# The order of the first burst of each unit: one score product and one transposed score product change places

## The chip, the cores and the metric

One NeuronCore of a Trainium2 chip runs the whole program in one launch. The metric is the device time in microseconds (us) of that core; of several runs the median counts. A core has a matrix engine (TensorE: PE for its matmuls, PEld for its weight loads), a vector engine (VectorE, DVE), a scalar engine (ScalarE, ACT), GpSimd (POOL), and a queue of its own for DMA transfers (SyncE, SP). Each has its own list of instructions and waits for the others by semaphores.

## What is computed

A transformer layer with attention and MLP side by side on one normalised input, 2048 rows of 512 values, 32 heads of 16:

```python
def _A_ref(x, wqkv, wo):
    qkv = (x @ wqkv).reshape(B, S, 3, H, Dh).transpose(2, 0, 3, 1, 4)
    q, k, v = qkv[0], qkv[1], qkv[2]
    scores = jnp.einsum("bhqd,bhkd->bhqk", q, k) * (Dh ** -0.5)
    p = _softmax(scores, axis=-1)
    o = jnp.einsum("bhqk,bhkd->bhqd", p, v)
    return o.transpose(0, 2, 1, 3).reshape(B, S, D) @ wo

def _B_ref(x, w1, b1, w2, b2):
    h = _gelu(jnp.einsum("bsd,df->bsf", x, w1) + b1)
    return jnp.einsum("bsf,fd->bsd", h, w2) + b2

xn = _layernorm(x)
return x + _A_ref(xn, wqkv, wo) + _B_ref(xn, w1, b1, w2, b2)
```

## The kernel before

The attention is cut into 8 groups of 4 heads (`NG`), 4 blocks of 512 queries (`NQB`) and 16 steps of 128 keys, so there are `NU` = 512 units. `unit(gen)` (line 745) writes the instructions of one unit. It works on two units at once: on unit u it takes the row maxima of the scores (queries on the partitions), and on unit e = u - 19 (`LEAD`) it does the softmax proper with the scores transposed (keys on the partitions). The maxima of a whole block of queries have to be known before its exponentials.

Three kinds of attention product stand in a unit, each for four heads n = 0 to 3:

- `s_half(u, n)`, line 366: the score product of head n into a PSUM bank named pS, and behind it on VectorE the row maximum (`s_max`, line 363, `mt<-pS` in the profile). Below it is called s0, s1, s2 or s3.
- `e_half(e, n)`, line 399: the transposed score product into a bank named pT, and behind it on ScalarE the exponential (line 410, `pe<-pT`). Below: e0 to e3.
- `v_half(w, r)`, line 413: the product of the exponentials with the values, for all four heads, summed in one bank named pV over 16 units. Line 436 copies it out on ScalarE (`osb<-pV`).

All of them use half the rows of the matrix array. Heads 0 and 2 use the low half (rows 0 to 63), heads 1 and 3 the high half (rows 64 to 127). Line 169 issues every product as four matmuls of 32 columns each (`tiled`, line 195), so eight small matmuls can be under way at once, four on each half. `v_half` takes one half of the rows in each half of a unit, and `dense` takes the other half of the rows: it issues three or four products on that half (`pace`) for whatever else has to be multiplied, which is the projection of q, k, v, the two MLP products and the output projection. These are the pD rows of the profile; each product is again four matmuls of 32 columns.

So a unit has two halves, a = 0 and a = 1, and each is a burst of four score products, then the values, then the dense products:

| | burst, in the order of the program | then |
|---|---|---|
| a = 0 | s0 (low), e1 (high), s1 (high), e0 (low) | values on high, dense on low |
| a = 1 | s2 (low), e3 (high), s3 (high), e2 (low) | values on low, dense on high |

Three things set waits around a burst. The first is the banks (line 102): scores rotate over three banks and transposed scores over three, so a product waits until the maximum or the exponential that read its bank three products earlier has ended. When a dense group ends and a new one begins, `dbank` (line 513) takes one of the T banks for it, and the bank of the old group joins the T banks only when ScalarE has read it (for the first MLP product in line 1312, `hh<-pD`). Until then the transposed scores have two banks. The values do the same with an S bank every 16 units.

The second is the `turns` semaphore (lines 167 to 194): values and dense products add into the same bank from both row halves in turn, so the first of them in a burst waits until the last of them in the burst before has ended. A dense group that is over is left out of that count.

The third is that all matmuls of TensorE count up one semaphore, in the order of the program. VectorE's maximum of s0 and ScalarE's exponential of e1 both wait for that count to reach a number.

Of the kernel before, what the change touches and what calls it, by code (L numbers as in the profile page):

```python
# [54 lines left out]
def layer_kernel(ctx: ExitStack, tc: tile.TileContext, x, wqkv, wo, w1, b1, w2, b2, out):  # L55
# [51 lines left out]
    def banks(tag):  # L107
        k = free_banks[tag].pop(0)
        free_banks[tag].append(k)
        return bank_tile(k, tag)  # L110
# [48 lines left out]
    def given(engine, ns):  # L159
        backlog[engine] += ns  # L160
# [17 lines left out]
    def leave(user, goes_on):  # L178

        p = newest.pop(user, None)  # L180
        if p is not None and goes_on:
            p.then_inc(turns, 1)
            tc.no_tile_sem_insts.add(p.ins.name)
            counted[0] += 1
            left.append(p)

    def enter():

        if left:
            goal[0] = f"turn{counted[0]}"  # L190
            for p in left:
                tc.add_to_no_dep_group(goal[0], p.ins)
            left.clear()

    def tiled(user, dst, lhs, rhs, start, stop):

        for j in range(0, P, 32):
            product(user, dst[j:j + 32], lhs[:, j:j + 32], rhs, start=start, stop=stop)
# [11 lines left out]
    def fetch_scale(m):  # L210

        scale_of[m] = nc.scalar.alloc_register(f"sexp{m}")
        nc.scalar.reg_load(scale_of[m], sexp[0:1, m:m + 1].bitcast(I32))

    class Plan:
# [7 lines left out]
        def add(self, engine, ns, fn, after=(), take=(), free=(), size=0, tail=0, gap=0):  # L223
            t = dict(gap=gap, e=engine, ns=ns, fn=fn, after=[a for a in after if a], take=take, free=free, size=size, tail=tail,
                     end=None, n=len(self.todo))
            for key in free:
                self.users.setdefault(key, []).append(t)
            self.todo.append(t)
            return t
# [89 lines left out]
    def tick():  # L319
        held[0] = pos[0] < NU and pos[0] % 16 == 0  # L320
        run_due()
        run_steps()
        slot[0] += 1
# [42 lines left out]
    def s_half(u, n):  # L366

        s = banks("S")
        s_mm(u, n, s)
        s_max(u, n, s)  # L370

    def s_end(u):

        t, i = divmod(u, 16)
        if i < 15:
            return
        g, qb = divmod(t, NQB)
        mneg = mnegs[t % 2]
        nc.vector.tensor_reduce(mneg[:, :16], mt_of[t].rearrange("p h t k -> p (h t) k"), axis=AX.X, op=ALU.max, negate=True)
        given("dve", 220)  # L380

        def store():

            pt = banks("S")
            for a in range(2):
                nc.tensor.matmul(pt[32 * a:32 * a + 32, :64], mneg[64 * a:64 * a + 64, :],
                                 ident[64 * a:64 * a + 64, 64 * a:64 * a + 64], start=True, stop=True)
            mhl = work.tile([64, 2, 64], F16, name="mhl", bufs=2)
            nc.vector.tensor_scalar_mul(mhl[:, 0], pt[:64, :64], 1.0 / MROW)
            nc.vector.scalar_tensor_tensor(mhl[:, 1], pt[:64, :64], 1.0 / MROW, mhl[:, 0], op0=ALU.mult, op1=ALU.subtract)  # L390
            given("dve", 300)
            for a in range(2):
                nc.sync.dma_start(m_d[t, :, :, 64 * a:64 * a + 64], mhl[32 * a:32 * a + 16])
            for h in range(4):
                m_rows(t, h)

        stores[t] = store

    def e_half(u, n):

        p, a = divmod(n, 2)
        t, kt = divmod(u, 16)
        g, qb = divmod(t, NQB)
        st = banks("T")
        r = slice(64 * a, 64 * a + 64)
        k0 = (kt % 4) * P
        tiled(None, st, kst[g % 2][kt // 4][r, p, k0:k0 + P], qst[g % 2][qb][r, p, :], True, True)
        pe = work.tile([P, QB], F32, name="pe", bufs=12)
        ptiles[u, n] = pe
        nc.scalar.activation(pe, st, AF.Exp, scale=scale_of[g // 2])  # L410
        given("act", 520)

    def v_half(u, a):

        t, kt = divmod(u, 16)
        g, qb = divmod(t, NQB)
        if kt == 0 and a == 0:
            pv_of[t] = hold("V", "S")
        pv = pv_of[t][0]
        r = slice(64 * a, 64 * a + 64)  # L420
        for h in (2, 3, 0, 1):
            c = (4 * g + h) * VW
            product("V", pv[32 * h:32 * h + 32, :], vv[r, kt, c:c + 32], ptiles[u, h][r],
                    start=(kt == 0 and a == 0), stop=(kt == 15 and a == 1))
# [77 lines left out]
    NU = NG * NQB * 16  # L502
# [155 lines left out]
    def ended(at_once=True):  # L658

        if cur[0] is not None and cur[0].over():  # L660
            done, cur[0] = cur[0], None
            ends.append(done.end)
            if at_once:
                settle()
# [5 lines left out]
    def one_more():  # L670

        if ends:
            ends.pop(0)()
        elif extras:
            extras.pop(0)()
# [10 lines left out]
    def dense(gen, side):  # L686

        f = group(gen)
        for _ in range(0 if f is None else f.pace[pos[0] % 2]):
            if not f.usable(side):  # L690
                return
            f.product(side)
# [25 lines left out]
    def spare(gen, side):  # L718

        if extra[0] is None and not spent[0]:  # L720
            f = next(gen, 0)
            spent[0] = f == 0
            extra[0] = Halves(f) if f else None
        if extra[0] is not None:
            extra[0].product(side)
            if extra[0].at == extra[0].n:
                extra[0] = None
# [17 lines left out]
    def unit(gen):  # L745


        u = pos[0]
        e = u - LEAD
        if e > 0 and e % (2 * NQB * 16) == 0 and e < NU:  # L750
            fetch_scale(e // (2 * NQB * 16))
        pos[0] += 1
        for a in range(2):
            for b in range(2 * a, 2 * a + 2):
                if u < NU:
                    s_half(u, b)
                elif u > NU:
                    spare(gen, b % 2)
                if 0 <= e < NU:
                    e_half(e, b ^ 1)  # L760
            if e >= 0:
                one_more()
                enter()

                w, r = (e - 2, 1) if a == 0 else (e - 1, 0)
                live = 0 <= w < NU
                new = r == 0 and w % 16 == 0
                if live and not new:
                    v_half(w, r)
                dense(gen, 1 - r)  # L770
                if live and new:
                    v_half(w, r)

                for user, goes_on in (("V", live and not (r == 1 and w % 16 == 15)),
                                      ("D", cur[0] is not None and not cur[0].over())):
                    leave(user, goes_on)
                for k in backlog:
                    backlog[k] = max(0, backlog[k] - HALF)
                if live and r == 1:
                    v_end(w)  # L780
                ended(False)

            if a == 0 and u % 16 == 0 and u // 16 - 1 in stores:
                stores.pop(u // 16 - 1)()
        if u < NU:
            s_end(u)
        tick()
# [9 lines left out]
    with ExitStack() as st1:  # L797
# [252 lines left out]
        for w in (1, 0):  # L1050
# [5 lines left out]
            else:  # L1056
                a = add("POOL", 800, lambda wf=wf, i1=i1: nc.gpsimd.tensor_scalar(tl[wf], tl[wf], i1, 0.0, op0=ALU.mult, op1=ALU.add), [h])
                w_ready[w] = add("POOL", 1100, lambda wf=wf, hi=hi, lo=lo: nc.gpsimd.tensor_tensor(lo, tl[wf], hi, op=ALU.subtract), [a], free=[wf])
        a = add("DVE", 90, lambda: nc.vector.tensor_tensor(sexp[:, 0:1], fac0[:, 0:1], fac0[:, 1:2], op=ALU.mult), [chain])
        a = add("DVE", 90, lambda: nc.vector.tensor_scalar_mul(sexp[:, 0:1], sexp[:, 0:1], DH ** -0.5), [a])  # L1060
# [5 lines left out]
        a = add("DVE", 90, lambda: nc.vector.tensor_tensor(amv[:, 2:3], amv[:, 0:1], amv[:, 1:2], op=ALU.max), v_sum)  # L1066
# [3 lines left out]
        for i in range(2):  # L1070
# [6 lines left out]
            else:  # L1077
                b = add("POOL", 1240, lambda key=key: nc.gpsimd.tensor_scalar(
                    tl[key], tl[key], inv_v[:, 0:1], 0.0, op0=ALU.mult, op1=ALU.add), [h])
# [30 lines left out]
        a = add("DVE", 220, maxima, m_last)  # L1110
# [3 lines left out]
        def turn_m():  # L1114
            tl[mkey] = sb_tile(mkey)
            for k in range(2):
# [3 lines left out]
        a = add("PE", 300, turn_m, [a], take=[mkey])  # L1120
        a = add("DVE", 160, lambda: nc.vector.tensor_scalar_mul(mhl[:, 0], tl[mkey][:64, :64], 1.0 / MROW), [a])
        a = add("DVE", 160, lambda: nc.vector.scalar_tensor_tensor(mhl[:, 1], tl[mkey][:64, :64], 1.0 / MROW, mhl[:, 0],
                                                                   op0=ALU.mult, op1=ALU.subtract), [a], free=[mkey])
# [371 lines left out]
```

## Time and profile before

| | |
|---|---|
| median of 3 runs | 1487.3 us (1486.66 to 1488.96) |
| the profiled execution, by its own time | 1485.57 us |
| its span, from the first to the last instruction | 1483.8 us |
| granted TensorE clock, mean | 0.997 |
| VectorE busy | 1374.5 us (93%), 2029 row maxima in it |
| ScalarE busy | 1259.2 us (85%), 2048 exponentials in it |
| GpSimd busy | 662.2 us (45%) |

Busy shares are unions over time of the instructions of an engine. For PE the ends of matmuls are modelled by the profiler, and a busy PE says nothing on its two row halves, of which one can stand still. A timeline row merges instructions of one kind that follow each other: start, length from the first start to the last end, engine, source line, the tiles, and xN for their number; in brackets stands idle time of the engine ahead of it and what ended it. Of the 2048 row maxima 2029 read a bank named pS; the other 19, of the prologue, read one named pV.

### The profile page before, as it was taken

To read this page: it belongs to the slowest core of one execution; us is meant where nothing else is said; L and a number is where in the kernel's file an instruction comes from. 1 tells how busy PE (TensorE), PEld (TensorE's weight loads), DVE (VectorE), ACT (ScalarE), POOL (GpSimd) and SP (SyncE) were. 2 spreads that over 40 slices of the span, in tenths; PEclk is the share of its full clock that TensorE was granted. 3 is DMA by queue.
4 is the path that set the end of the run, shared out by engine and by line. 5 is a ranking of instruction groups with operands and counts; after the bars stand their busy time and mean duration, and the time that the engine had idled before them with its cause. 6 is when DMAs were issued, how large, how long until landed. Compare 5 with 4: busy or idle time off the path is not lost.

```text
span 1483.8 us, 88118 instructions
## 1 busy us (share of the span) xinstructions
PE 1467.1 (99%) x40158; PEld 811.5 (55%) x40158; DVE 1374.5 (93%) x2305; ACT 1259.2 (85%) x2366; POOL 662.2 (45%) x672
## 2 busy tenths in 40 slices
PE   8999999999999999999999999999999999999998
PEld 4445555555555555555555555555555555555554
DVE  7889999999999999999999999999999999999923
ACT  5868888888999888899988889998888998888884
POOL 3202857563787301377831037782115777121100
PEclk9999999999999999999999999999999999999999
DMA  6732556554224210221112111121112110111432
GB/s 213 226 113 70 163 171 195 160 157 144 76 72 114 65 37 23 68 62 41 44 43 87 30 36 44 53 73 44 43 38 80 50 37 21 56 55 31 141 93 95
DMA packets 112623, 124.83 MB, mean 84 GB/s; under 512 B 22908, under 2 KB 84220, under 8 KB 112248
## 3 DMA queue, kind: packets, MB, share of 16 engines
q1 hardware_dynamic: 112248, 119.18, 26.6%
q8 instruction: 314, 5.14, 1.5%
q14 instruction: 61, 0.50, 0.1%
HBM read 81.66 MB, written 37.34 MB: 80 GB/s over the span
## 4 chain that ended last, share of the span: by engine, by line
PE 89%; DVE 8%; ACT 1%; DMA 1%; issue 0%; SPq 0%; DVEq 0%; ACTq 0%
PE pV L169 26%; PE pD L169 25%; PE pS L169 18%; PE pT L169 18%; DVE mt L363 7%; PE pT L992 2%; DMA wq<-in_A_wqkv_dram 1%; PE pD L992 0%; DVE ac L1370 0%; ACT xs L945 0%; PE pT L962 0%; ACT xt L966 0%; DVE xt L975 0%; SPq L858 0%; DVE wvh L1075 0%
## 5 line engine op out<-in xcount | busy, mean ns | idle before, releaser
L363 DVE TENSOR_REDUCE mt<-pS 128x1 f32<-128x512 f32 x2029 | 1296.9, 684 | 44.0 <-PE pS L169 24.3
L410 ACT ACTIVATE pe<-pT 128x512 f32<-128x512 f32 x2048 | 1111.5, 599 | 178.0 <-PE pT L169 84.4
L169 PE MATMUL pV<-pe,vv 64*32 64x512 f32 x8192 | 1072.3, 594 | 0.1
L169 PE MATMUL pT<-qst,kst 64*32 64x512 f16 x8192 | 709.8, 378 | 0.5 <-issue 0.5
L169 PE MATMUL pS<-kst,qst 62*32 62x512 f16 x8116 | 614.3, 378 | 3.6 <-DVE mt L363 2.2
L169 PEld LDWEIGHTS <-qst 62*32 62x32 f16 x8192 | 283.6, 92 | 237.5 <-issue 58.0
L169 PE MATMUL pD<-xb,wc 64*32 64x512 f16 x5376 | 360.9, 377 | 0.0
L169 PEld LDWEIGHTS <-kst 64*32 64x32 f16 x8192 | 269.8, 91 | 159.9 <-issue 69.2
L169 PE MATMUL pD<-w_s,g 64*32 64x512 f16 x5376 | 356.4, 377 | 0.0
L169 PEld LDWEIGHTS pV<-pe,vv 64*32 64x32 f32 x8192 | 182.0, 105 | 88.9 <-PE pV L169 4.5
L169 PE MATMUL pD<-xt,wqk_h 64*32 64x512 f16 x2400 | 157.8, 378 | 0.0
L169 PEld LDWEIGHTS <-wc 64*32 64x32 f16 x5376 | 117.0, 91 | 43.0 <-issue 0.6
L169 PEld LDWEIGHTS <-g 64*32 64x32 f16 x5376 | 113.8, 92 | 41.0
L1337 POOL TENSOR_TENSOR xa<-xa,yt 128x512 f32<-128x512 f32 x16 | 20.4, 1278 | 232.0 <-ACT yt L1335 232.0
L466 POOL TENSOR_TENSOR osb<-osb,rb 128x512 f32<-128x512 f32 x31 | 39.8, 1283 | 165.8 <-DMA rb<-den_d 123.4
L1289 POOL TENSOR_TENSOR t<-hh 128x512 f32<-128x512 f32 x56 | 58.2, 1040 | 86.3 <-ACT hh L1312 85.3
L1291 POOL TENSOR_TENSOR t<-t,hh 128x512 f32<-128x512 f32 x56 | 71.7, 1281 | 4.7
L1284 POOL TENSOR_TENSOR t<-t,hh 128x512 f32<-128x512 f32 x56 | 71.7, 1281 | 4.7
L1283 POOL TENSOR_SCALAR t<-t,gs 128x512 f32<-128x512 f32 x56 | 38.7, 692 | 66.0 <-ACT t L1278 66.0
L1286 POOL TENSOR_TENSOR g<-t,g 128x512 f16<-128x512 f32 x56 | 65.2, 1163 | 4.7
L169 PEld LDWEIGHTS <-wqk_h 64*32 64x32 f16 x2400 | 54.5, 92 | 19.4 <-issue 1.4
L169 PE MATMUL pD<-wo_s,oc 64*32 64x512 f16 x828 | 54.7, 378 | 0.0
(160 smaller groups left out, 874.8 us busy)
## 6 DMA issues: line engine op xcount, KB each, us to landing
wc<-w_d SPq DMA_DIRECT2D x56, 256.0 KB
qk_d<-stg SPq DMA_DIRECT2D x32, 256.0 KB
rb<-den_d SPq DMA_DIRECT2D x124, 64.0 KB
wch<-in_B_w_dram SPq DMA_DIRECT2D x14, 512.0 KB
wch<-in_B_w_dram SPq DMA_DIRECT2D x28, 256.0 KB
w_d<-wsp SPq DMA_DIRECT2D x28, 256.0 KB
kst<-qk_d SPq DMA_DIRECT2D x64, 96.0 KB
qst<-qk_d SPq DMA_DIRECT2D x64, 96.0 KB
```

The costliest lines, as they stand in the source:

```text
L169: p = nc.tensor.matmul(*args, **kw)
L363: nc.vector.reduce_max(mt_of[t][:, n, qt, kb:kb + 1], s, axis=AX.X)
L410: nc.scalar.activation(pe, st, AF.Exp, scale=scale_of[g // 2])
L466: pooled((1280, lambda: nc.gpsimd.tensor_tensor(osb, osb, rb, op=ALU.mult)), (620, lambda: nc.gpsimd.tensor_scalar(ot[:, 0], osb, 1.0, 0.0 ...
L992: nc.tensor.matmul(tl[key], lhs, rhs, start=c + n == 0, stop=(c, n) == (NC - 1, 2))
L1283: pooled((690, lambda: nc.gpsimd.tensor_scalar(t1, t1, 1.0, gs[:, 1:2], op0=ALU.add, op1=ALU.mult)), (1280, lambda: nc.gpsimd.tensor_tenso ...
L1284: (1280, lambda: nc.gpsimd.tensor_tensor(t1, t1, hh, op=ALU.mult)),
L1286: (1160, lambda: nc.gpsimd.tensor_tensor(g[:, 1, f, :], t1, g[:, 0, f, :], op=ALU.subtract)),
L1289: pooled((1040, lambda: nc.gpsimd.tensor_tensor(t1, hh, hh, op=ALU.mult)), (620, lambda: nc.gpsimd.tensor_scalar(t1, t1, 1.0, 1.0 / GELU_A ...
L1291: (1280, lambda: nc.gpsimd.tensor_tensor(t1, t1, hh, op=ALU.mult)),
L1337: add = lambda: nc.gpsimd.tensor_tensor(xa, xa, yt, op=ALU.add)
```

## The change

In the first half of a unit, e1 moves ahead of s0. The second half is written in another way and keeps its order.

```diff
         for a in range(2):
-            for b in range(2 * a, 2 * a + 2):
-                if u < NU:
+            for kind, b in ((1, 1), (0, 0), (0, 1), (1, 0)) if a == 0 else ((0, 2), (1, 3), (0, 3), (1, 2)):
+                if kind and 0 <= e < NU:
+                    e_half(e, b)
+                elif not kind and u < NU:
                     s_half(u, b)
-                elif u > NU:
+                elif not kind and u > NU:
                     spare(gen, b % 2)
-                if 0 <= e < NU:
-                    e_half(e, b ^ 1)
             if e >= 0:
```

Kind 1 is a transposed score, kind 0 a score. The new order of the first half is e1 (high), s0 (low), s1 (high), e0 (low).

TensorE, the first half of a unit in the MLP's second product. In the rows, `pS<-kst,qst` is a score, `pT<-qst,kst` a transposed score, the LDWEIGHTS ahead of each is its weight load, and "waits DVE" or "waits Activation" is the wait for the bank to be read by that engine; of each product the first of its four matmuls is shown. Before:

```order
L169 MATMUL pD<-w_s,g 32x512
L169 LDWEIGHTS qst_1_88
L169 MATMUL pS<-kst_3_82,qst_1_88 32x512 [waits DVE_49]
...
L169 LDWEIGHTS kst_0_79 [waits DMAHW4_49]
L169 MATMUL pT<-qst_0_87,kst_0_79 32x512 [waits Activation_49]
...
L169 MATMUL pS<-kst_3_82,qst_1_88 32x512 [waits DVE_49]
...
L169 MATMUL pT<-qst_0_87,kst_0_79 32x512 [waits Activation_49]
...
L169 MATMUL pV<-pe,vv 32x512 [waits turns]
```

TensorE at the same place with the change:

```order
L169 MATMUL pD<-w_s,g 32x512
L169 LDWEIGHTS kst_0_79 [waits DMAHW4_49]
L169 MATMUL pT<-qst_0_87,kst_0_79 32x512 [waits Activation_49]
...
L169 LDWEIGHTS qst_1_88
L169 MATMUL pS<-kst_3_82,qst_1_88 32x512 [waits DVE_49]
...
L169 MATMUL pS<-kst_3_82,qst_1_88 32x512 [waits DVE_49]
...
L169 MATMUL pT<-qst_0_87,kst_0_79 32x512 [waits Activation_49]
...
L169 MATMUL pV<-pe,vv 32x512 [waits turns]
```

The four weight loads and four matmuls of e1, with the wait for ScalarE and here with a wait for a transfer of the keys, went ahead of s0; nothing else moved.

TensorE, the first half of a unit that comes after the sum of the values was copied out (30 of these). Before:

```order
L169 MATMUL pV<-pe,vv 32x512 [waits DVE_49]
L169 MATMUL pV<-pe,vv 32x512 x3
L169 LDWEIGHTS qst_1_92
L169 MATMUL pS<-kst_1_84,qst_1_92 32x512 [waits Activation_49]
...
L169 LDWEIGHTS kst_0_83
L169 MATMUL pT<-qst_0_91,kst_0_83 32x512
```

With the change:

```order
L169 MATMUL pV<-pe,vv 32x512 [waits DVE_49]
L169 MATMUL pV<-pe,vv 32x512 x3
L169 LDWEIGHTS kst_0_83
L169 MATMUL pT<-qst_0_91,kst_0_83 32x512 [waits Activation_49]
...
L169 LDWEIGHTS qst_1_92
L169 MATMUL pS<-kst_1_84,qst_1_92 32x512 [waits Activation_49]
```

Here s0 takes the bank that ScalarE just copied out. Before, its wait covered that of e1; now e1 has a wait of its own ahead of it. The lists of VectorE, ScalarE, GpSimd and SyncE, with what they wait for, are the same in both programs.

## The prediction

> **What bounds the kernel now.** I read the page first, then the stretch of 100 to 1400 us by windows, then the waits of ScalarE, then single bursts in the timeline.
>
> ```profile
> PE 1467.1 (99%) x40158; PEld 811.5 (55%) x40158; DVE 1374.5 (93%) x2305; ACT 1259.2 (85%) x2366; POOL 662.2 (45%) x672
> PE 89%; DVE 8%; ACT 1%; DMA 1%; issue 0%; SPq 0%; DVEq 0%; ACTq 0%
> 100.00:1400.00 1300.00, 1017.27 (x7772) 172.30 (x7768) 0.00 (x0) 18.19 (x30) 1.00 0.25 74
> 100.00:1400.00 1300.00, 925.99 (x13928) 0.00 (x0) 0.00 (x0) 69.41 (x106) 1.00 0.25 74
> ACT pe L410 <- PE pS L169: 69.6, 286, 0.6
> L169 PE MATMUL pS<-kst,qst 62*32 62x512 f16 x8116 | 614.3, 378 | 3.6 <-DVE mt L363 2.2
> ```
>
> The first row is the page's, the second its chain of waits: TensorE holds 89% of it and VectorE 8%. The third row is the windows view of the values alone (pV): 7772 matmuls at 16 a unit are 486 units in 1300 us, 2.68 us a unit and 1.34 us a burst. The fourth is the same for the dense bank (pD): 13928 matmuls are 14.3 a burst, so bursts have 12 or 16 of them, and ScalarE read a dense bank 106 times, so 106 times a dense group ended. The fifth row is odd and is what the change touches: exponentials, which read pT, waited 286 times for a product that writes pS, 69.6 us in all. The last row is the page's on score matmuls, 0.38 us each by the profile's model, and TensorE hardly waits ahead of them.
>
> Two bursts show why, and what paces a burst. First one with 12 dense matmuls:
>
> ```profile
> 385.91 0.61 PE L169 MATMUL pD<-xb,wc 64*32 64x512 f16 x8
> 386.32 0.61 PE L169 MATMUL pV<-pe,vv 64*32 64x512 f32 x4
> 386.35 0.39 PE L169 MATMUL pD<-xb,wc 64*32 64x512 f16 x4
> 386.57 0.39 PE L169 MATMUL pT<-qst,kst 64*32 64x512 f16 x4
> 386.75 0.42 PE L169 MATMUL pS<-kst,qst 62*32 62x512 f16 x8
> 386.97 0.39 PE L169 MATMUL pT<-qst,kst 64*32 64x512 f16 x4
> 387.15 0.63 PE L169 MATMUL pV<-pe,vv 64*32 64x512 f32 x4
> 387.21 0.69 DVE L363 TENSOR_REDUCE mt<-pS 128x1 f32<-128x512 f32 x1
> 387.33 1.08 ACT L410 ACTIVATE pe<-pT 128x512 f32<-128x512 f32 x2 [0.28 <-PE pS L169]
> ```
>
> This is a first half. In the program s0 comes ahead of e1, yet e1 started at 386.57 and s0 with s1 at 386.75: the values held the low half till then, the high half was free earlier, and e1 went ahead by itself. But its exponential started at 387.33, 0.12 behind the maximum of s0, and the idle 0.28 is put down to pS: the products end for the others in the order of the program. Then the pace. The values started at 386.32 and ended by the profile at 386.93; the next values came 0.22 later, though s1 left the high half at about 386.75 + 0.21 = 386.96 (a product holds a half for some 0.21, as from 386.75 to 386.97 on the low half).
>
> ```profile
> 656.45 0.61 PE L169 MATMUL pV<-pe,vv 64*32 64x512 f32 x4
> 656.46 0.60 PE L169 MATMUL pD<-xb,wc 64*32 64x512 f16 x8
> 656.88 0.39 PE L169 MATMUL pT<-qst,kst 64*32 64x512 f16 x4
> 656.89 0.59 PE L169 MATMUL pS<-kst,qst 62*32 62x512 f16 x8
> 657.12 0.39 PE L169 MATMUL pT<-qst,kst 64*32 64x512 f16 x4
> 657.33 0.59 PE L169 MATMUL pV<-pe,vv 64*32 64x512 f32 x1
> ```
>
> With 16 dense matmuls (eight more stand ahead of these) it is 657.33 - 657.06 = 0.27, and here both halves are full too: 657.12 + 0.21 = 657.33. Where the dense group was over and drops out of the turn it is 669.02 - 668.94 = 0.08 (rows below). So the turn from values to values, with its dense matmuls behind it, sets the burst: (0.22 - 0.08) / 12 = 0.012 us for each dense matmul that has still to be ended in order, and (0.27 - 0.22) / 4 = 0.012 again. **The order of the four products does not stand on that turn**, nor does it change how long either half is full.
>
> **Where it can matter** is a bank wait. A unit in which a dense group changes:
>
> ```profile
> 668.33 0.61 PE L169 MATMUL pV<-pe,vv 64*32 64x512 f32 x4
> 668.57 0.39 PE L169 MATMUL pT<-qst,kst 64*32 64x512 f16 x4
> 668.76 0.42 PE L169 MATMUL pS<-kst,qst 62*32 62x512 f16 x8
> 669.02 0.63 PE L169 MATMUL pV<-pe,vv 64*32 64x512 f32 x4
> 669.33 1.09 ACT L410 ACTIVATE pe<-pT 128x512 f32<-128x512 f32 x2 [0.28 <-PE pS L169]
> 669.98 0.40 PE L169 MATMUL pT<-qst,kst 64*32 64x512 f16 x4
> 670.06 0.54 PE L169 MATMUL pS<-kst,qst 62*32 62x512 f16 x8
> 670.30 0.69 ACT L1312 ACTIVATE hh<-pD,b_s 128x512 f32<-128x512 f32 x1
> 670.47 0.40 PE L169 MATMUL pT<-qst,kst 64*32 64x512 f16 x4
> 670.68 0.61 PE L169 MATMUL pV<-pe,vv 64*32 64x512 f32 x4
> ```
>
> The values at 669.02 and at 670.68 are 1.66 apart, not 1.34. The new dense group holds a T bank and hh has not yet freed the old one, so e3 needs the bank of e1 and e2 that of e0. The exponential of e1 ran from 669.33 to 669.93 and e3 started at 669.98; that of e0 ended at 669.33 + 1.09 = 670.42 and e2 started at 670.47. Each instant by which the exponential of e1 starts sooner is one by which this burst ends sooner.
>
> **The change part by part.** It adds and removes nothing: on TensorE e1's four weight loads and four matmuls go ahead of s0's, in 486 units or so between 100 and 1400 us, and past no other queue. No DMA moves. Its parts:
>
> 1. Start of e1, s0 and s1: nothing. e1 went first already (386.57 before 386.75), or together with s0 where both halves were full.
>
> 2. The exponential of e1, sooner. It need not wait for the end of s0, but it does wait for what stands ahead of it: values and dense matmuls of the burst before. In the unit above the values ended at 668.94, 12 dense matmuls behind them take 12 x 0.012 = 0.14, and the four matmuls of e1 0.05: 669.13. Before, s0 ended at 668.76 + 0.38 = 669.14 (the 0.38 of the page's row), and its four and e1's four had to be ended after that: 669.24. So 0.11 sooner. With 16 dense matmuls the row of 656.89 shows score and transposed score starting together; then only the order of ending is left, four matmuls or 0.05, less where the dense matmuls end last. Bounds: 0.01 a unit, one matmul's ending, and 0.28, the whole idle time in the rows. I take 0.05, nearer to the full bursts, since dense matmuls average 14.3 and the full burst is the commoner one.
>
> 3. Where that counts: not in an ordinary unit, where ScalarE has idle time (85%) that hides it, but in the 106 with a change of the dense group: 106 x 0.05 = **5.3 us gained** (bounds 106 x 0.01 = 1.1 and 106 x 0.28 = 29.7).
>
> 4. The maximum of s0, later: its count now has e1's four matmuls ahead, 0.05 at most. VectorE has slack for it in most units (93% busy, 8% of the chain). It counts where the values take a bank from the scores, once per block of 16 units, the 30 copies in the third row of the first fence: 30 x 0.05 = **1.5 us lost** (bounds 0, and 486 x 0.05 = 24.3 if VectorE decided everywhere).
>
> 5. e1's wait for its T bank now stands ahead of s0 in TensorE's queue; behind it stand s0, s1, e0, the values and the dense products, and VectorE waits for s0. Taken at nothing: three banks back is an exponential of the unit before, and e1 at 386.57 or 668.57 was not held. If it were held, s0's wait for VectorE would no longer hold e1 in turn.
>
> The sum against the profiled execution: 1485.57 (its span 1483.8 and 1.8 around it) - 5.3 + 1.5 = 1481.8; against the median of the runs, which is 1.7 above that execution, 1487.3 - 3.8 = 1483.5, rounded to **1484 us**.
>
> The row that speaks first on order is e1 at 386.57 ahead of s0 at 386.75. The Trainium skill, "TensorE: Matmul & The Clock Gate", Part 3 on packing small matmuls, states that matmuls start and end strictly in program order. By it e1 would have been held behind s0, and the change would let it start 0.18 sooner. The trace contradicts the half on starts and agrees with the half on ends (exponential 387.33 behind maximum 387.21).
>
> **The rivals.** *A larger gain.* The exponential of e1 is not held by dense matmuls of the burst before, and the idle time goes nearly whole: 106 x 0.15 to 0.28 is 16 to 30 us, about 1467. For it speaks the row of 69.6 us; against it the turn, which does grow with the dense matmuls.
>
> *Starts in program order.* If the trace's starts were misread and e1 is held by s0, high-half work moves up by 0.18 a unit. The values still wait for their turn, so only full bursts gain, and there both halves are full: 0.05 x 243, half the units, or 12 us, 1475. The rows speak against it. This is the page's rule as a result of its own.
>
> *Nothing.* The gain goes into the next wait of the same burst (e2's bank needs hh or e0, whose own product ends later), 1487.
>
> *Slower: e1's bank wait holds s0.* In the first half after a group change ScalarE is behind by the copy of the dense bank (670.30, 0.69), and the exponential of e3 starts only at 670.87. If it ends after the values leave the low half, s0 is now held behind e1, and VectorE and the score banks with it. It decides from the point where e3's exponential ends later than the second values row plus 0.43, here about 671.48 against 671.54, so it is close. One exponential, 0.60, in a quarter of the 106 units is 16 us, less the gain of 5: 1498. Against it: before, e1 was held at that place too, and the high half with it.
>
> **How the numbers follow.** The forecast of a small gain has 0.44; the larger gain 0.11; starts in order 0.03; nothing 0.15; slower 0.27. What a measurement of this kernel can tell from no change is about 0.2%, 3 us. Of the forecast 0.28 lies beyond that and 0.16 within, so faster is 0.28 + 0.11 + 0.03 = 0.42; same is 0.16 + 0.15 + 0.02 of small losses = 0.33; slower 0.25. The forecast's own range is 1480 to 1487. The range for 8 in 10 takes half of the larger gain and most of the slower case: 1473 to 1496.
>
> **What would show it.** In the profile of the changed kernel the wait of exponentials for pS should fall from 69.6 us and the exponential of e1 should start ahead of, or with, the maximum of s0. Values 1.66 apart in a group change should come 0.05 to 0.11 closer, and the turns of 0.22 and 0.27 in ordinary bursts stay. Wrong: if ordinary bursts change, part 1 or 4 has failed; if VectorE's share of the chain rises well above 8%, part 4; if the weight loads of s0 show new idle time in units after a group change, part 5; if the group changes come 0.2 closer, the hold by dense matmuls is wrong.

## The result, and the profile after

The changed kernel takes 1480.33 us (median of 6 runs, 1479.38 to 1484.19); before it is 1487.35 us over 6 runs. The ratio is 0.9955, 95% interval 0.9945 to 0.9966: 7 us faster. The profiled execution has a span of 1477.7 us instead of 1483.8.

From the page of the changed kernel, its windows view of the values (100 to 1400 us) and the waits of ScalarE:

```profile
PE 1459.2 (99%) x40158; PEld 813.4 (55%) x40158; DVE 1359.3 (92%) x2305; ACT 1260.1 (85%) x2366; POOL 662.3 (45%) x672
PE 91%; DVE 6%; ACT 2%; DMA 1%; issue 1%; SPq 0%; DVEq 0%; ACTq 0%
100.00:1400.00 1300.00, 1021.57 (x7800) 172.01 (x7800) 0.00 (x0) 18.06 (x30) 1.00 0.25 75
ACT pe L410 <- PE pS L169: 91.8, 370, 1.5
```

The work is the same: the busy times of ScalarE and GpSimd stay, those of PE and VectorE fall by 8 and 15 us. The 1300 us hold 7800 matmuls of the values instead of 7772. VectorE's share of the chain fell from 8% to 6%. The last row went the other way than expected, from 69.6 to 91.8 us; what it means is taken up below.

The same group change as in the prediction, in the changed kernel's timeline (first start, length, xN; the VectorE row is the maximum of s0):

```profile
666.45 0.61 PE L169 MATMUL pV<-pe,vv 64*32 64x512 f32 x4
666.69 0.39 PE L169 MATMUL pT<-qst,kst 64*32 64x512 f16 x4
666.88 0.42 PE L169 MATMUL pS<-kst,qst 62*32 62x512 f16 x8
667.15 0.63 PE L169 MATMUL pV<-pe,vv 64*32 64x512 f32 x4
667.37 0.69 DVE L363 TENSOR_REDUCE mt<-pS 128x1 f32<-128x512 f32 x1
667.38 1.08 ACT L410 ACTIVATE pe<-pT 128x512 f32<-128x512 f32 x2 [0.20 <-PE pS L169]
668.03 0.39 PE L169 MATMUL pT<-qst,kst 64*32 64x512 f16 x4
668.51 0.40 PE L169 MATMUL pT<-qst,kst 64*32 64x512 f16 x4
668.73 0.61 PE L169 MATMUL pV<-pe,vv 64*32 64x512 f32 x4
```

The matmuls stand as before: e1 leads s0 by 0.19 us in both kernels, though it now also does so in the program. The exponential of e1 started 667.38 - 667.06 = 0.32 us after the second pass of the values ended by the profile (666.45 + 0.61); before, it was 669.33 - 668.94 = 0.39. The idle time ahead of it is 0.20 instead of 0.28. e3 follows the end of that exponential (667.38 + 0.60) by 0.05 and e2 that of e0's (667.38 + 1.08) by 0.05, as before, so the two rows of values are 668.73 - 667.15 = 1.58 apart instead of 1.66. The gain is 0.08 us in this unit. The wait of e2 is that of nearly all such units: in the trace before, e2 started 0.03 to 0.08 us after the end of e0's exponential in 96 of the 112 units that begin with a new dense group, and in 6 of 396 others.

Lining up the starts of the values in the two traces, burst by burst, gives where the 6.1 us of the spans went. Second halves: 100 bursts became more than 0.04 us shorter, 8.6 us together, and 92 of them lie in the 112 units with a new dense group; all other bursts, of both halves, lost 3.4 us together, most of it by a few large differences in both directions in the first hundred bursts. Counted without that choice, the second halves of the 112 units became 7.1 us shorter, 0.063 us each. The program reached its first values 0.9 us sooner; this difference is there at the first row maximum (32.6 instead of 33.5 us) already, ahead of anything that the change touches. The mean burst that ends a first half is the same, 1.28 us in both.

### The profile page after: what moved, and what is told of

It is laid out like the page before. It is cut to its first block, busy times and chain, and to the rows that moved or that the text cites. A ratio compares the mean times of both kernels' runs of the same rounds, so it can differ in the third digit from the quotient of the medians.

```text
span 1477.7 us, 88118 instructions
## 1 busy us (share of the span) xinstructions
PE 1459.2 (99%) x40158; PEld 813.4 (55%) x40158; DVE 1359.3 (92%) x2305; ACT 1260.1 (85%) x2366; POOL 662.3 (45%) x672
## 4 chain that ended last, share of the span: by engine, by line
PE 91%; DVE 6%; ACT 2%; DMA 1%; issue 1%; SPq 0%; DVEq 0%; ACTq 0%
PE pV L169 27%; PE pD L169 25%; PE pT L169 18%; PE pS L169 18%; DVE mt L363 4%; PE pT L992 2%; DMA wq<-in_A_wqkv_dram 1%; PE pD L992 0%; DVE ac L1370 0%; DVE xt L975 0%; ACT xs L945 0%; ACT pe L410 0%; ACT hh L1312 0%; ACT wqk_h L881 0%; DVE wvh L1075 0%
## 5 line engine op out<-in xcount | busy, mean ns | idle before, releaser
L363 DVE TENSOR_REDUCE mt<-pS 128x1 f32<-128x512 f32 x2029 | 1282.0, 684 | 54.8 <-PE pS L169 24.3
L410 ACT ACTIVATE pe<-pT 128x512 f32<-128x512 f32 x2048 | 1111.5, 599 | 171.6 <-PE pS L169 91.8
L169 PE MATMUL pS<-kst,qst 62*32 62x512 f16 x8116 | 607.6, 378 | 3.2 <-DVE mt L363 2.0
```

The lines of the kernel that those rows point to most:

```text
L169: p = nc.tensor.matmul(*args, **kw)
L363: nc.vector.reduce_max(mt_of[t][:, n, qt, kb:kb + 1], s, axis=AX.X)
```

## The experiments

**The place.** Two kernels make the swap in a part of the units only: where the dense group is over when the unit begins, and where it is not. With `fresh = cur[0] is None` at the start of `unit`, the first:

```diff
-            for kind, b in ((1, 1), (0, 0), (0, 1), (1, 0)) if a == 0 else ((0, 2), (1, 3), (0, 3), (1, 2)):
+            for kind, b in ((1, 1), (0, 0), (0, 1), (1, 0)) if a == 0 and fresh else ((0, 0), (1, 1), (0, 1), (1, 0)) if a == 0 else ((0, 2), (1, 3), (0, 3), (1, 2)):
```

> The swap is made only in the 112 units whose dense group is over when the unit begins, so that a new one takes a T bank in its first half; the other 380 keep the old order. Theory (the exponential of e1 starts some 0.08 us sooner, and that counts only where the T banks are scarce): the whole gain, 6 to 7 us, about 1481 us, ratio 0.9955. Rival (every changed unit gains a little, 7 us / 492 = 0.014 us each, for instance because TensorE's queue moves better): 112 x 0.014 = 1.6 us, about 1486 us.

Measured: 1479.86 us, ratio to before 0.9954 (0.9940 to 0.9967). The second kernel has `not fresh` at that place.

> The swap is made only in the 380 units in which the dense group goes on; the 112 with a new group keep the old order. Theory: nothing, 1487 us within 1.5 us; the exponential of e1 starts sooner here too and ScalarE's idle time hides it. Rival (a little in every unit): 380 x 0.014 = 5.3 us, about 1482 us.

Measured: 1487.84 us beside 1486.77 us before, ratio 1.0007 (0.9998 to 1.0016). In 112 units the swap gives the whole gain; in the other 380 it gives nothing that can be told from the spread of the runs. The exponentials of e1 moved in the second kernel's other units too, by 0.06 us in the median, and those bursts did not get shorter.

**The second half as well.** The second half begins with its transposed score too:

```diff
-... else ((0, 2), (1, 3), (0, 3), (1, 2)):
+... else ((1, 3), (0, 2), (0, 3), (1, 2)):
```

> The first half as in the changed kernel, and the second half too begins with its transposed score: e3, s2, s3, e2. Theory (products start by themselves when their half of the rows is free, only their ends are in order): s2 still starts ahead of e3, its maximum comes about 0.04 us later, the exponential of e3 0.05 us sooner, which only counts where T banks are scarce in a first half; 1478 to 1481 us, the changed kernel's time within 2 us. Rival (starts in program order): e3's half is busy with the values 0.19 us longer, so s2 is held that long in the bursts with 12 dense matmuls, some 200 of the second halves, up to 38 us slower, about 1500 to 1518 us.

Measured: 1481.55 us, ratio 0.9958 (0.9942 to 0.9973), the changed kernel's within the intervals. Its timeline, a second half:

```profile
385.31 0.60 PE L169 MATMUL pV<-pe,vv 64*32 64x512 f32 x3
385.54 0.39 PE L169 MATMUL pS<-kst,qst 62*32 62x512 f16 x4
385.74 0.59 PE L169 MATMUL pT<-qst,kst 64*32 64x512 f16 x8
```

s2 stands behind e3 in the program and starts 0.20 us ahead of it, as soon as the low half is free. Here a product whose half is busy does not hold the next one on the other half.

**The cost enlarged.** The first half in the order s0, s1, e1, e0:

```diff
-... in ((1, 1), (0, 0), (0, 1), (1, 0)) if a == 0 ...
+... in ((0, 0), (0, 1), (1, 1), (1, 0)) if a == 0 ...
```

> The suspected cost is enlarged: first half s0, s1, e1, e0, so that s1 goes ahead of e1 on the high half. Theory: e1 starts 0.21 us later than before the change and its exponential ends up about 0.2 us later; the 112 units with a new dense group lose that each, 112 x 0.2 = 22 us, about 1510 us; the length of both halves is the same. Rival (the order within a burst does not matter and the gain had another cause): 1487 us.

Measured: 1499.51 us, ratio 1.0075 (1.0059 to 1.0091): slower by 12.7 us, about half of what was expected. The timeline of a unit with a new dense group, the burst before which has 16 dense matmuls:

```profile
667.27 0.59 PE L169 MATMUL pV<-pe,vv 64*32 64x512 f32 x3
667.70 0.40 PE L169 MATMUL pS<-kst,qst 62*32 62x512 f16 x8
667.92 0.41 PE L169 MATMUL pT<-qst,kst 64*32 64x512 f16 x8
668.44 1.08 ACT L410 ACTIVATE pe<-pT 128x512 f32<-128x512 f32 x2 [0.45 <-PE pT L169]
669.08 0.40 PE L169 MATMUL pT<-qst,kst 64*32 64x512 f16 x4
669.57 0.40 PE L169 MATMUL pT<-qst,kst 64*32 64x512 f16 x4
```

e1 starts a product later than s1 (667.92 after 667.70), and the exponential comes 668.44 - 667.86 = 0.58 us after the end of the values, against 0.42 before as the median of bursts with 16 dense matmuls. This unit is one of the worst: over all first halves the median went from 0.42 to 0.53, 0.11 later and not 0.2, and it is 0.10 in the 112 units. The start of e1 did move as far as expected, by 0.21 us behind 16 dense matmuls and by 0.30 behind 12; the exponential moved by 0.14 and 0.06 only. Before, it had come later than e1's own start would have let it, held by what stands ahead of e1 in the program. 112 x 0.11 is 12 us. The waits of e3 and e2 for the two exponentials are there again (669.08 after 668.44 + 0.60, 669.57 after 668.44 + 1.08).

**What else holds the exponential.** The prediction had the dense matmuls of the burst before end ahead of e1, in the order of the program. The next kernels issue one, two or all of a burst's dense products ahead of the values, and the rest behind (`dense` got bounds `lo` and `hi` on its loop):

```diff
+                dense(gen, 1 - r, 0, 1)
                 if live and not new:
                     v_half(w, r)
-                dense(gen, 1 - r)
+                dense(gen, 1 - r, 1)
```

> The changed kernel, with one of the three or four dense products of a burst issued ahead of the values instead of behind them (same work, same sums; not where a new sum of values begins, which has the dense products first anyway). Theory (matmuls end in the order of the program, 0.012 us each, so values are followed by 12 or 16 endings before the turn, and before e1 can be reported): four endings fewer, the turn after 12 dense matmuls falls from 0.22 to about 0.17 us and the exponential of e1 starts 0.05 us sooner again; some 300 bursts with 12 dense matmuls get 0.03 to 0.05 us shorter and 100 group changes 0.05: 1480 - 10 to 20 us, 1460 to 1470 us. Rival (the turn is the delay of the semaphore alone, and dense matmuls ahead of the values only hold those back in the queue): the turn stays, values start 0.03 us later, 1480 to 1500 us.

Measured: 1467.53 us, ratio 0.9857 (0.9841 to 0.9874).

> As before with two dense products ahead of the values. Theory: eight endings fewer, turn 0.12 us after 12 dense matmuls; but the weights of the second product can only be loaded when the first has started, so the values may be dispatched up to 0.1 us late; between 1455 and 1480 us, better than with one only if the late dispatch is hidden. Rival: slower than with one, 1490 us and more.

Measured: 1462.31 us, ratio 0.9823 (0.9807 to 0.9840), the fastest kernel here, 26 us below the 1488.10 measured beside it before the change.

> As before with all dense products ahead of the values. Theory: the turn falls to 0.08 us, the length without dense endings, but the values are dispatched only when the last but one dense product has started, 0.4 us late in each of some 970 bursts, of which VectorE and the other half hide part: 1600 us and more. Rival (TensorE takes matmuls of a free half from any depth of its queue): about 1450 us.

Measured: 1477.95 us, ratio 0.9930 (0.9910 to 0.9950). Neither number of this one came; all products ahead is slower than two, yet faster than none. Its timeline shows that the values were not late:

```profile
700.35 0.40 PE L169 MATMUL pS<-kst,qst 62*32 62x512 f16 x4
700.47 0.62 PE L169 MATMUL pV<-pe,vv 64*32 64x512 f32 x4
700.57 0.62 PE L169 MATMUL pD<-xb,wc 64*32 64x512 f16 x8
```

In the program the dense products now stand ahead of the values, yet the values started first, 0.10 us ahead: the high half, on which these dense products run, was held by s3 until about 700.35 + 0.21. In 274 of 977 bursts of this trace the values started ahead of all 12 dense matmuls. In 622, with 16, they started 0.03 us behind the first four (median) and ahead of the other twelve; in none did they pass more than 12. The expected delay of 0.4 us rested on values that cannot pass dense products.

Bursts of 12 dense matmuls, from the timeline with one product ahead and then with two:

```profile
387.40 0.61 PE L169 MATMUL pV<-pe,vv 64*32 64x512 f32 x4
388.20 0.64 PE L169 MATMUL pV<-pe,vv 64*32 64x512 f32 x4
```

```profile
386.52 0.61 PE L169 MATMUL pV<-pe,vv 64*32 64x512 f32 x4
387.30 0.63 PE L169 MATMUL pV<-pe,vv 64*32 64x512 f32 x4
```

The turn from the end of values to the next values was 0.22 us; it is 388.20 - 388.01 = 0.19 with four dense matmuls fewer behind the values and 387.30 - 387.13 = 0.17 with eight fewer, 0.006 to 0.008 us for each. The exponential of e1 came 0.39 us after the end of the values before, 0.32 in the changed kernel, 0.28 with one product ahead, 0.25 with two and 0.21 with all (of all first halves the value that one in ten stays below). So the endings of dense matmuls do stand ahead of e1, at 0.008 to 0.010 us each, a little less than the 0.012 reckoned.

**Whether the swap still counts there.** With two products ahead, the swap undone, and then made only at a new dense group:

```diff
-... in ((1, 1), (0, 0), (0, 1), (1, 0)) if a == 0 ...
+... in ((0, 0), (1, 1), (0, 1), (1, 0)) if a == 0 ...
```

> The kernel with two dense products ahead of the values (1462 us), with the order of this change undone: first half s0, e1, s1, e0 again. Theory: with eight dense endings fewer behind the values, the exponential of e1 was held less by them and more by s0, so undoing the change costs at least what the change gave, 7 us, and up to 0.19 us in each of 112 group changes, 21 us: 1469 to 1483 us. Rival (the earlier turn already gave what the change gives): within 2 us of 1462 us.

Measured: 1472.91 us, ratio 0.9900 (0.9884 to 0.9917): 10.6 us slower than with the swap (1462.31 us, measured at another time).

> The same kernel with two dense products ahead of the values, the new order only in the 112 units with a new dense group. Theory: the place is the same as before, so 1462 us within 2 us. Rival (with shorter bursts the exponential of e1 or the maximum of s0 matters in ordinary units as well): 1465 us or more if e1 does, 1460 us or less if s0 does.

Measured: 1463.89 us, ratio 0.9840 (0.9823 to 0.9856), the same as 1462.31 within the intervals. It is 9.0 us below the kernel with the swap undone that ran beside it. The place is again the group change. With fewer dense matmuls behind the values the swap moved the exponential of e1 further: in the 112 units from 0.40 to 0.28 us after the end of the values (medians), against 0.40 to 0.34 without products ahead. That it is worth more there, 9 to 11 us instead of 7, agrees with this, but the difference is hardly clear of the spread of the runs.

## Why the prediction was right, point by point

*What bounds the kernel* held. Ordinary bursts kept their time: the swap made in 380 of the units changed nothing, and moving dense endings off the turn made their bursts shorter (with two products ahead by some 12 us in all units without a new dense group, in the traces).

*Part 1, starts unchanged,* held: at the group change shown e1 is ahead of s0 by 0.19 us before and after. The trace and the third experiment contradict the rule of starts in program order that the prediction weighed; the rival built on it, 1475 us, did not come, though the time is not far from it.

*Part 2, the exponential of e1 sooner,* held, and its size was a little small: "I take 0.05, nearer to the full bursts". Over all first halves the median went from 0.416 to 0.357 us after the end of the values, 0.06. Behind 16 dense matmuls it was 0.06 (0.419 to 0.360; 0.05 reckoned), behind 12 it was 0.08 (0.399 to 0.320; 0.11 reckoned). About half of the 112 units have 16 behind the values, so the full burst was a fair choice. The larger gain, 0.15 to 0.28 us in each of these units, did not come: the hold by dense matmuls is there, as the kernels with fewer of them behind the values show.

*Part 3, only at a change of the dense group,* held, in the sharpest way: 112 units give all, 380 give none. The count, 106 assumed and 112 found, was near.

*Part 4, a loss of 1.5 us by s0's later maximum,* did not come. The maximum did come later, by 0.06 us in the median (0.293 to 0.353 us after the end of the values), more than the 0.05 allowed. At a block boundary the values do wait for it: a burst there went from 1.365 to 1.425 us, and the median of all 31 from 1.402 to 1.442. But the next one went from 1.243 to 1.180 (median 1.243 to 1.182), so the block got it back at once.

*Part 5, e1's bank wait ahead of s0,* was rightly taken at nothing; the slower rival, 1498 us, did not appear. The first halves' mean burst is unchanged, and in the units right after a group change the first half kept its length (median difference 0.000 us) and s0 its start (0.001).

So the sum should have been 112 x 0.063 = 7.1 us gained and nothing lost at the boundaries; the runs give 7 us where it said 3.8 and rounded to 3. Of the difference 1.8 us belong to part 2 with its count, and 1.5 to part 4. The way, the place and the mechanism were right, the size was about half. What the other bursts of the two traces lost, and what was won ahead of the first values, leave about 1 us between them; the runs do not explain it, and the runs of one kernel differ by up to 5 us from one to the next.

*What would show it:* values at the group change shown came 0.08 closer, within 0.05 to 0.11 (the median of the 112 is 0.06), and the turns of 0.22 and 0.27 stayed. One sign was wrong: the waits of exponentials "for pS" were to fall, and rose from 69.6 to 91.8 us. The releaser's name in that row is that of the matmul whose report came last by the profile's reckoning, and since all matmuls count up one semaphore it need not be the one whose bank is read. In the changed kernel e1's exponential starts 0.01 us behind the maximum of s0 instead of 0.12, though s0 no longer stands ahead of it in the program; what holds it now are the endings ahead of e1. All idle time ahead of exponentials, whatever the name, fell from 178.0 to 171.6 us by the two pages. The distance between the two rows said what the total in the waits view could not.

## What to carry to other kernels

Where instructions of one engine are reported in program order (here by one semaphore that all of them count up), put the one whose reader is short of buffers first among those that end together; it costs nothing where, as here, each starts as soon as its half of the rows is free. Look for the few places where that reader is late (here 112 of 492 units), since elsewhere its idle time takes any gain. And look at what is reported ahead of a turn that everybody waits for: moving two of the three or four dense products ahead of the values was worth another 18 us on top of the swap.

## What the runs showed of the hardware that was not expected

Matmuls on the two row halves start out of program order by up to 0.2 us, in both directions (e1 ahead of s0 before the change, s2 ahead of e3 in the third experiment), while what waits for them sees them end in program order: the exponential of e1 came 0.12 us behind the maximum of s0 before, though e1 had started 0.18 us ahead of it. The report of each dense matmul that stands ahead costs 0.008 to 0.010 us, which adds up to a tenth of a microsecond for the 12 dense matmuls of a burst. With all dense products ahead of the values a gain remained, 10 us below before, where a loss of over 100 us had been expected: values started ahead of up to 12 dense matmuls that precede them in the program and wait for the other half. They never started ahead of more than 12; whether that is as far as TensorE's queue reaches was not tested.
